# Attention with a gated feed-forward gate on one core: down and output products in whole PSUM banks

## The chip, the core and the metric

The kernel runs on one core of a Trainium2 chip. The metric is device time in microseconds (us) of one execution; the time shown for a kernel is the median of several executions on the same chip, beside which the profile describes one more execution, taken by the hardware profiler. PE is the matrix engine, DVE the vector engine, ACT the activation engine, POOL and SP are used here for small work and for starting transfers.

## What is computed

All inputs are bf16; the sequence has 2048 rows of 640 columns, 32 heads of 20 columns, and a feed-forward width of 1728.

```
xn  = layernorm(x)                         # no weights
q, k, v = split(xn @ wqkv)                 # 32 heads of 20
s   = softmax(q k^T / sqrt(20)) v  @ wo
h   = sigmoid(xn @ w_gate) * (xn @ w_up)
g   = silu(h @ w_down)
out = x + s * g
```

## The kernel before

**Layout.** After a setup that normalises x and transposes it into `xnT`, the queries are cut into four chunks of 512 rows (QC), and the heads into eight groups of four (NG = 8, 32 rows of the partition dimension per head). A pass is one group of heads for one chunk: 32 passes, each of 64 score banks (128 keys x 512 queries of one head, one PSUM bank of 512 fp32 columns). `kT_all` holds K of all groups, 2048 bf16 columns a group; `v_all` holds V.

**Exponentials on two engines.** The 2048 score banks are the bulk of the work. ACT takes two or three banks in one activation (`act_exp`, L1305), out of two sets of PSUM banks. DVE takes single banks: PE writes the scores to one of two banks called `misc0` and `misc1`, DVE clamps them into an SBUF pair (`dy`, L1325), which frees the bank, and when two banks are together it makes the power of two of them with three passes over 1024 columns (L1346, L1350, L1356). The result `p` of either engine is multiplied by V on PE (L1482) into the bank `oacc`. The last group of the last chunk is done in three parts (`PARTS`, `last_job`), with an epilogue that ends the kernel.

**The same two banks serve the jobs.** Everything else that PE does is a job, a generator that asks for a bank, issues its matmuls one at a time into the gaps between scores, and hands DVE or ACT what has to be done with the bank: projections of Q, K and V, `gateup_job` (54 pairs of products into `hT`; the tanh of the gate is on ACT at L679 and the product on DVE at L688, from two banks), `down_job`, `out_job`, `part_job`. At most two jobs are in flight (MOST).

**Who sets the order.** The order of all instructions is made when the program is built: a planner keeps a clock for PE, ACT and DVE (`pe[0]`, `act`, `dve`) from costs written by hand (MM5 = 216 ns for a matmul of 512 columns, MM3 = 136 for 320, 606 for a DVE pass over 512, 400 over 320, 740 over 640), and always issues what would start next. Jobs are sorted by a due time counted in score banks (`STAGE_END`, `OUT_DUE`, `PART_DUE`). A bank is free once the planner's time of the last reader has passed. `issue` and `alone` (from L1240 on) choose whether DVE gets a bank of scores: when a `misc` bank is free and DVE's backlog is under a limit. `zero_add` (L1453 to L1467) issues matmuls on zeros when too little has been streamed by PE in the last 3.4 us of the planner's clock; they go into `oacc` between its own matmuls (L1458), or into a free `misc` bank (L1464). On the chip each engine runs its list in order and waits at semaphores.

**The down product** (`down_job`, L695) runs once for each of 16 tiles of 128 rows, when `hT` of the chunk is whole. Two halves of 320 columns, 14 matmuls each (L709), take one bank after the other; DVE copies each half into `d2` (L713); ACT makes the tanh of all 640 columns (L720, `td`), and DVE makes `gq = (tanh + 1) * d2` (L725). For chunks 0 to 2, POOL starts the write of it to `gq_dram` (L729). In the last chunk it stays, in the memory of K's group t4, which has to be done with by then.

**The output product** (`out_job`, L737) runs for the 12 tiles of chunks 0 to 2, one chunk later. SP starts the load of the gate (L743); two halves, eight matmuls each (L748), take a bank each; DVE multiplies with the gate (L754), and after the second half POOL starts a DMA that adds the tile to `out`, where x was copied before (L757). A tile waits for the tile before it.

**The last chunk.** `part_job` (L767) sums the first five groups' part of the output product in advance, multiplies it with the gate (L787) into `ahead`, which lies in the memory of `hT`, and adds x by a DMA (L790). `near_job` and `last_job` add the last groups.

**The normalisation** of a pass (`normalise`, L796) sends the row sums through memory: POOL starts a write of the sums (L807), a load (L812), after DVE's reciprocal (L816) a write (L817) and four loads (L823); then DVE scales the result (L835).

Of the kernel before, what the change touches and what calls it, by code (L numbers as in the profile page):

```python
# [15 lines left out]
P = 128  # L16
# [42 lines left out]
def kernel(  # L59
# [38 lines left out]
    gq_dram = dram.tile([TT, P, D], FP32, name="gq_dram", tag="gqd")  # L98
# [268 lines left out]
    WINDOW, ENOUGH, ZEROS = 3400.0, 2500.0, 16  # L367
# [327 lines left out]
    def down_job(tt):  # L695
        c, t4 = divmod(tt, QC // P)
        yield "known", lambda: (bulk[0] == NFT and pe[0] > bulk_t[0] + LANDED and len(h_cells.get(c, [])) == NFT and (tt < 2 or tt - 2 in gq_cells)
                                and (c < NQC - 1 or front() >= PER_PASS * (NG * c + t4 + 1)))
        yield "wait", h_cells[c] + ([gq_cells[tt - 2]] if tt > 1 else [])
        hT = hTs[c]  # L700
        d2 = glu[0].tile([P, D], FP32, tag="gqr", bufs=4, name="d2")
        got = []
        for h in range(2):
            e0_, e1_ = h * HALF, (h + 1) * HALF
            held, psd = yield "bank",
            for kf in range(NFT):
                rows = slice(0, P) if kf < NFT - 1 else slice(EDGE * (c % 2), EDGE * (c % 2 + 1))
                h_in = hT[:, kf, :] if kf < NFT - 1 else hEs[c]
                nc.tensor.matmul(psd[:, 0:HALF], lhsT=h_in[rows, t4 * P:(t4 + 1) * P],  # L709
                                 rhs=glu[1][rows, kf, e0_:e1_], start=(kf == 0), stop=(kf == NFT - 1))  # L710
                yield "mm", MM3
            got.append(dve.add(400.0, [Cell(pe[0] + PE_OUT)], lambda psd=psd, e0_=e0_, e1_=e1_:
                               nc.vector.tensor_copy(out=d2[:, e0_:e1_], in_=psd[:, 0:HALF]), 1))  # L713
            give_bank(held, got[-1])
# [3 lines left out]
        def tanh():  # L718
            made["t"] = glu[0].tile([P, D], BF16, tag="td", bufs=1, name="td")
            nc.scalar.activation(out=made["t"], in_=d2, func=ACT.Tanh, scale=0.25)  # L720

        def finish():
            last = c == NQC - 1
            gq = kT_all[:, t4, :].bitcast(FP32)[:, 0:D] if last else d2
            nc.vector.scalar_tensor_tensor(out=gq, in0=made["t"], scalar=1.0, in1=d2, op0=ALU.add, op1=ALU.mult)  # L725
            if last:
                gq_last[t4] = gq
            else:
                nc.gpsimd.dma_start(out=gq_dram[tt, :, :], in_=d2)  # L729
# [3 lines left out]
        gq_cells[tt] = td_free[-1]  # L733

    td_free, tnh_free, gq_cells, out_cells = [], [], {}, {}

    def out_job(tt):  # L737
        qc, t4 = divmod(tt, QC // P)
        yield "known", lambda: (bulk[1] > tt and all((qc, g) in ot_cells for g in range(NG))
                                and (not tt or tt - 1 in out_cells))  # L740
        yield "wait", [ot_cells[qc, g] for g in range(NG)] + ([out_cells[tt - 1]] if tt else [])
        gqr = glu[0].tile([P, D], FP32, tag="gqr", bufs=4, name="gqr")
        nc.sync.dma_start(out=gqr, in_=gq_dram[tt, :, :])  # L743
        landed = Cell(pe[0] + 3000.0)
        for h in range(2):
            held, pss = yield "bank",
            for g in range(NG):
                nc.tensor.matmul(pss[:, 0:HALF], lhsT=oTs[qc, g][:, t4 * P:(t4 + 1) * P],  # L748
                                 rhs=wo_pad[:, g, h * HALF:(h + 1) * HALF], start=(g == 0), stop=(g == NG - 1))
                yield "mm", MM3  # L750

            def finish(h=h, pss=pss):
                half = gqr[:, h * HALF:(h + 1) * HALF]
                nc.vector.scalar_tensor_tensor(out=half, in0=pss[:, 0:HALF], scalar=0.25, in1=half,  # L754
                                               op0=ALU.mult, op1=ALU.mult)
                if h == 1:
                    nc.gpsimd.dma_start(out=out_view[:, tt, :], in_=gqr, accum_op=ALU.add)  # L757

            done = dve.add(400.0, [Cell(pe[0] + PE_OUT), landed], finish, 1)
            give_bank(held, done)  # L760
        out_cells[tt] = done

    gq_last, ahead = {}, []
# [3 lines left out]
    def part_job(t4):  # L767
        tt = (NQC - 1) * 4 + t4
        gqs = range((NQC - 1) * 4, NQC * 4)
        yield "known", lambda: (all((NQC - 1, g) in ot_cells for g in range(PRE))  # L770
                                and all(x in gq_cells for x in gqs) and tt - 1 in out_cells)
        yield "wait", [ot_cells[NQC - 1, g] for g in range(PRE)] + [gq_cells[x] for x in gqs] + [out_cells[tt - 1]]
# [848 lines left out]
```

## Time and profile before

| | |
|---|---|
| median of 3 runs | 883.36 us (883.22 to 884.05) |
| profiled execution | 887.23 us |
| its span, first to last instruction | 885.3 us |
| granted PE clock, mean of the span | 0.996 |
| instructions | 16801 |
| moved by DMA | 63.85 MB |

A group line of the profile reads: line, engine, operation, output and inputs with their shapes, count, then the engine's busy time in the group, the mean ns of one, and the idle time of the engine just before them with what ended it. A row of a stretch gives the stretch's length and then the busy us and, in brackets, the instructions of PE, PE's weight loads (PEld), DVE, ACT and POOL, the granted PE clock (1.00 is full), the share of DMA time and GB/s. A row in the order of time gives start, duration, engine, line and operation, with the idle time before it in square brackets. A duration includes the latency of the instruction, so that neighbours on one engine overlap.

### The profile page before, as it was taken

The page shows a single profiled execution, that of the slowest core. Times are in us where ns is not written, and L with a number is a line of the kernel's source. Part 1 is how long each engine was busy: PE and PEld are TensorE (multiplying, and loading weights), DVE is VectorE, ACT ScalarE, POOL GpSimd, SP SyncE. Part 2 cuts the span into 40 slices and gives each one's busy share as a digit, 9 for nine tenths or more (in the row PEclk, how much of TensorE's full clock was granted, in tenths as well). Part 3 has the DMA queues.
Part 4 walks back from the last instruction along what each step waited for, and adds up shares of the span by engine and source line. Part 5 has one row for each costly group of instructions (what it writes and reads, how often), then busy time and mean ns, then how long its engine had stood idle before and what let it go on. Part 6 is the DMA issues. An engine that isn't in the chain of part 4 may idle for free.

```text
span 885.3 us, 16801 instructions
## 1 busy us (share of the span) xinstructions
PE 806.4 (91%) x6388; PEld 293.1 (33%) x6469; DVE 849.1 (96%) x1210; ACT 864.1 (98%) x828; POOL 158.4 (18%) x299
## 2 busy tenths in 40 slices
PE   7998999899998999999989998999999898999996
PEld 3434333332222333222223332223233232233344
DVE  7799999999999899999999999999999999999997
ACT  7999999999999899999999999999999999999996
POOL 8401111110111112111101132101112021111110
PEclk9999999999999899999999999999999999999999
DMA  8212231115642024223321234312202252200030
GB/s 318 61 51 63 72 106 36 44 55 141 159 131 58 20 83 94 50 58 73 68 56 50 79 66 87 71 38 68 62 29 87 75 86 71 72 22 20 6 69 31
DMA packets 104902, 63.85 MB, mean 72 GB/s; under 512 B 77618, under 2 KB 99206, under 8 KB 104730
## 3 DMA queue, kind: packets, MB, share of 16 engines
q1 hardware_dynamic: 94838, 46.96, 19.7%
q0 software_dynamic: 9984, 15.83, 7.8%
q8 instruction: 50, 0.82, 0.4%
q14 instruction: 30, 0.25, 0.1%
HBM read 49.94 MB, written 16.11 MB: 75 GB/s over the span
## 4 chain that ended last, share of the span: by engine, by line
ACT 52%; issue 17%; DVE 17%; PE 9%; DMA 2%; POOL 1%; SPq 0%; DVEq 0%; ACTq 0%; POOLq 0%
ACT p L1305 49%; DVE dy L1325 4%; DVE p L1356 3%; DVE du L1350 3%; DVE du L1346 3%; PE sc L1279 3%; ACT tnh L679 2%; PE work L709 2%; PE oacc L1482 2%; DMA den<-den_dram 1%; PE work L667 1%; DMA x_sb<-in_A_x_dram 1%; DVE d L713 1%; DVE stats L261 1%; DVE oT L835 1%
## 5 line engine op out<-in xcount | busy, mean ns | idle before, releaser
L1305 ACT ACTIVATE p<-sc 128x1536 bf16<-128x1536 f32 x711 | 818.9, 1344 | 5.7 <-PE sc L1279 3.2
L1279 PE MATMUL sc<-qT,kT_all 21*128 21x512 bf16 (+2 forms) x1892 | 278.5, 370 | 51.7 <-ACT p L1305 46.6
L1325 DVE TENSOR_SCALAR dy<-spare 128x512 f32<-128x512 f32 x271 | 184.8, 682 | 9.2 <-PE spare L1279 7.9
L1279 PEld LDWEIGHTS <-kT_all 21*128 21x128 bf16 x2176 | 89.0, 91 | 290.0 <-issue 278.2
L1346 DVE SCALAR_TENSOR_TENSOR du<-dy 128x1024 f32<-128x1024 uint16 (+1 forms) x170 | 170.1, 1002 | 2.5
L1350 DVE SCALAR_TENSOR_TENSOR du<-du,dy 128x1024 f32<-128x1024 f32 (+1 forms) x166 | 169.1, 1019 | 0.9
L1356 DVE SCALAR_TENSOR_TENSOR p<-du,dy 128x1024 uint16<-128x1024 f32 (+1 forms) x150 | 166.7, 1111 | 1.0
L1482 PE MATMUL oacc<-p,v_all 128*21 128x512 bf16 (+2 forms) x2176 | 157.2, 371 | 0.5 <-issue 0.3
L1279 PE MATMUL spare<-qT,kT_all 21*128 21x512 bf16 (+2 forms) x284 | 104.0, 374 | 1.7 <-DVE dy L1325 0.8
L807 POOL DMA_DIRECT2D den_dram<-oev x30 | 17.4, 582 | 368.2 <-DVE oev L803 357.2
L667 PE MATMUL work<-xnT,wg 128*128 128x512 bf16 (+1 forms) x262 | 73.3, 382 | 3.7 <-DVE dy L1325 1.0
L709 PE MATMUL work<-wd,hT 128*128 128x320 bf16 x416 | 74.7, 306 | 1.6 <-DVE dy L1325 0.9
L667 PE MATMUL work<-xnT,wu 128*128 128x512 bf16 (+1 forms) x265 | 70.7, 381 | 2.9 <-DVE dy L1325 1.2
L823 POOL DMA_DIRECT2D rl<-rec_dram x120 | 60.7, 535 | 54.7 <-DMA rec_dram<-den 47.8
L1458 PE MATMUL oacc<-xnT,zero 128*128 128x512 bf16 x147 | 50.9, 386 | 2.8 <-issue 2.5
L1482 PEld LDWEIGHTS <-v_all 128*21 128x21 bf16 x2176 | 31.9, 90 | 59.6 <-issue 56.3
L709 PEld LDWEIGHTS <-hT 128*128 128x128 bf16 x416 | 34.6, 99 | 37.2 <-issue 26.5
L817 POOL DMA_DIRECT2D rec_dram<-den x30 | 16.4, 548 | 129.6 <-DVE den L816 129.6
L679 ACT ACTIVATE tnh<-work 128x512 bf16<-128x512 f32 x54 | 37.6, 696 | 0.0
L667 PEld LDWEIGHTS <-wu 128*128 128x128 bf16 (+1 forms) x280 | 23.8, 98 | 38.0 <-issue 20.2
L688 DVE SCALAR_TENSOR_TENSOR hT<-tnh,work 128x512 bf16<-128x512 bf16 x52 | 35.3, 678 | 0.3 <-ACT tnh L679 0.2
L748 PE MATMUL work<-wo_pad,oT 128*128 128x320 bf16 x192 | 34.3, 301 | 0.8 <-DVE dy L1325 0.5
(133 smaller groups left out, 579.1 us busy)
## 6 DMA issues: line engine op xcount, KB each, us to landing
wg<-in_B_w_gate_dram SPq DMA_DIRECT2D x52, 160.0 KB
wu<-in_B_w_up_dram SPq DMA_DIRECT2D x52, 160.0 KB
rl<-rec_dram POOLq DMA_DIRECT2D x120, 64.0 KB, 2.4
qT<-q_dram SPq DMA_DIRECT2D x31, 128.0 KB
gq_dram<-d POOLq DMA_DIRECT2D x12, 320.0 KB, 2.5
gqr<-gq_dram SPq DMA_DIRECT2D x12, 320.0 KB
kT_all<-k_dram SPq DMA_DIRECT2D x28, 128.0 KB
wd<-in_B_w_down_dram SPq DMA_DIRECT2D x13, 160.0 KB
```

Of the source, the lines that this page charges most:

```text
L667: nc.tensor.matmul(ps[EDGE * k:EDGE * (k + 1), :] if both else ps, lhsT=w[:, kd, 0:EDGE if both else P], rhs=xnT[:, kd, (c + k) * QC:(c + ...
L679: nc.scalar.activation(out=made["t"][0:fsz, :], in_=psg[0:fsz, :], func=ACT.Tanh, scale=0.5)
L709: nc.tensor.matmul(psd[:, 0:HALF], lhsT=h_in[rows, t4 * P:(t4 + 1) * P], rhs=glu[1][rows, kf, e0_:e1_], start=(kf == 0), stop=(kf == NFT - 1))
L823: nc.gpsimd.dma_start(out=t["rl"][32 * j:32 * j + 32, :], in_=rec_dram[n, j:j + 1, :].to_broadcast([32, QC]))
L1279: nc.tensor.matmul(ps[:, c0:c0 + n], lhsT=kT_all[rows, g, kt * P:(kt + 1) * P], rhs=qTs[qc, g][rows, q0:q0 + n], start=True, stop=True, ti ...
L1305: nc.scalar.activation(out=buf.tile(), in_=ps, func=ACT.Exp, bias=EXP_BIAS, scale=exp_scale)
L1325: nc.vector.tensor_scalar(out=pair.y[:, i * 512:(i + 1) * 512], in0=ps, scalar1=LEAST, scalar2=None, op0=ALU.max)
L1346: nc.vector.scalar_tensor_tensor(out=t["u"][:, a:e], in0=t["f"][:, a:e], scalar=CUBE_2, in1=t["f"][:, a:e], op0=ALU.add, op1=ALU.mult)
L1350: nc.vector.scalar_tensor_tensor(out=t["u"][:, a:e], in0=t["u"][:, a:e], scalar=CUBE_1, in1=t["f"][:, a:e], op0=ALU.add, op1=ALU.mult)
L1356: nc.vector.scalar_tensor_tensor(out=t["p"][:, a:e], in0=t["u"][:, a:e], scalar=CUBE_SCALE, in1=t["y"][:, a:e], op0=ALU.mult, op1=ALU.add)
L1458: nc.tensor.matmul(oacc, lhsT=zero, rhs=xnT[:, 0, 0:QC], start=not begun, stop=not begun, skip_group_check=True)
L1482: nc.tensor.matmul(oacc[32 * j:32 * j + 1 + Dh, q0:q0 + width], lhsT=v_all[:, kt, GH * g + j, 0:1 + Dh], rhs=buf.ap[:, i, c0:c0 + width], ...
```

## The change

The down and the output product are cut into banks instead of tiles. The four tiles of a chunk have 4 x 640 = 2560 columns side by side, which are five banks of 512; `down_pieces(k)` lists which columns of which tiles fall into bank k (one piece of 512; 128 + 384; 256 + 256; 384 + 128; 512). For each of 20 banks `down_job(c, k)` issues 14 matmuls for each piece, ACT makes the tanh straight from PSUM, and DVE makes the gate from the tanh and PSUM; the copies and `d2` are gone, and the bank is given back after the gate. `td` shares the buffers of the gate-up's `tnh`. Before, a job waited for the gate of two tiles earlier; now it doesn't. The output product has 15 banks instead of 24 halves; the gate is loaded by banks (`gq_dram` has the new shape), the planner lets 1.4 us pass after the load is started before it asks for a bank, and each piece is added to `out` by a DMA of its own.

In the last chunk the gates (`gq_last`) fill the first 10 KB a partition of K's memory (groups 0 to 2), and `ahead` the next 10 KB (groups 2 to 4), no longer `hT`'s memory; `part_job` may start one pass earlier, waits only for the gates of its own tile, and is due 24 banks earlier. `zero_add` takes a `misc` bank only when it has been free for 400 ns of the planner's clock. The planner's costs follow.

```diff
-    gq_dram = dram.tile([TT, P, D], FP32, name="gq_dram", tag="gqd")
+    gq_dram = dram.tile([NQC, P, 4 * D], FP32, name="gq_dram", tag="gqd")
...
-    WINDOW, ENOUGH, ZEROS = 3400.0, 2500.0, 16
+    WINDOW, ENOUGH, ZEROS, RESTED = 3400.0, 2500.0, 16, 400.0
...
-            yield "known", lambda: len(d_cells.get(c - 1, [])) == QC // P
+            yield "known", lambda: len(d_cells.get(c - 1, [])) == D // P
...
+    def mm_time(n):
+        return max(n / 2.4 + 3.0, 100.0)
+
+    def down_pieces(k):
+        return [(t4, max(t4 * D, k * QC), min((t4 + 1) * D, (k + 1) * QC)) for t4 in range(QC // P)
+                if t4 * D < (k + 1) * QC and (t4 + 1) * D > k * QC]
+
+    def down_job(c, k):
+        last = c == NQC - 1
+        yield "known", lambda: (bulk[0] == NFT and pe[0] > bulk_t[0] + LANDED and len(h_cells.get(c, [])) == NFT
+                                and (not last or front() >= PER_PASS * (NG * c + k // 2 + 1)))
+        yield "wait", h_cells[c]
...
+        held, psd = yield "bank",
+        for t4, f0, f1 in down_pieces(k):
             for kf in range(NFT):
...
+                nc.tensor.matmul(psd[:, f0 - k * QC:f1 - k * QC], lhsT=h_in[rows, t4 * P:(t4 + 1) * P],
+                                 rhs=glu[1][rows, kf, f0 - t4 * D:f1 - t4 * D], start=(kf == 0), stop=(kf == NFT - 1),
+                                 skip_group_check=True)
+                yield "mm", mm_time(f1 - f0), (f1 - f0) / 2.4
...
-            made["t"] = glu[0].tile([P, D], BF16, tag="td", bufs=1, name="td")
-            nc.scalar.activation(out=made["t"], in_=d2, func=ACT.Tanh, scale=0.25)
+            made["t"] = wk.tile([P, QC], BF16, tag="tnh", bufs=2, name="td")
+            nc.scalar.activation(out=made["t"], in_=psd, func=ACT.Tanh, scale=0.25)
...
-            nc.vector.scalar_tensor_tensor(out=gq, in0=made["t"], scalar=1.0, in1=d2, op0=ALU.add, op1=ALU.mult)
...
+            nc.vector.scalar_tensor_tensor(out=gq, in0=made["t"], scalar=1.0, in1=psd, op0=ALU.add, op1=ALU.mult)
+            if not last:
+                nc.gpsimd.dma_start(out=gq_dram[c, :, k * QC:(k + 1) * QC], in_=gq)
...
-        turned = act.add(590.0, got + td_free[-1:], tanh, 0, EXP_LAG)
-        td_free.append(dve.add(740.0, [turned], finish, 2))
+        turned = act.add(480.0, [Cell(pe[0] + PE_OUT + 100.0), *tnh_free[-2:-1]], tanh, 0, EXP_LAG)
+        tnh_free.append(dve.add(606.0, [turned], finish, 1))
+        give_bank(held, tnh_free[-1])
...
+    def out_job(qc, k):
+        cut = down_pieces(k)
...
+        nc.sync.dma_start(out=gqr, in_=gq_dram[qc, :, k * QC:(k + 1) * QC])
         landed = Cell(pe[0] + 3000.0)
+        yield "wait", [Cell(pe[0] + 1400.0)]
+        held, pss = yield "bank",
+        for t4, f0, f1 in cut:
             for g in range(NG):
...
+            nc.vector.scalar_tensor_tensor(out=gqr, in0=pss, scalar=0.25, in1=gqr, op0=ALU.mult, op1=ALU.mult)
+            for t4, f0, f1 in cut:
+                nc.gpsimd.dma_start(out=out_view[:, qc * 4 + t4, f0 - t4 * D:f1 - t4 * D],
+                                    in_=gqr[:, f0 - k * QC:f1 - k * QC], accum_op=ALU.add)
...
+    gq_last = kT_all[:, 0:3, :].rearrange("p g s -> p (g s)").bitcast(FP32)[:, 0:4 * D]
+    ahead = kT_all[:, 0:5, :].rearrange("p g s -> p (g s)").bitcast(FP32)[:, 4 * D:8 * D].rearrange(
+        "p (t d) -> p t d", d=D)
...
-    GU_COST, DOWN_COST = 10 * MM5, 2 * NFT * MM3
-    OUT_COST, PART_COST = 2 * NG * MM3, 2 * (NG - 3) * MM3
-    PART_DUE = [LAST-24 + 8 * t4 for t4 in range(4)]
+    GU_COST, DOWN_COST = 10 * MM5, NFT * (MM5 + 10.0)
+    OUT_COST, PART_COST = NG * (MM5 + 10.0), 2 * (NG - 3) * MM3
+    PART_DUE = [LAST-48 + 8 * t4 for t4 in range(4)]
...
-        jobs.append(Job(part_job(t4), PART_COST, len(steps) - 2, PART_DUE[t4]))
+        jobs.append(Job(part_job(t4), PART_COST, len(steps) - 3, PART_DUE[t4]))
...
-            free = [i for i in range(2) if banks[i].t is not None and banks[i].t <= pe[0]]
+            free = [i for i in range(2) if banks[i].t is not None and banks[i].t <= pe[0] - RESTED]
```

More of the change, by code (lines that the diff above doesn't have):

```diff
@@ L693, in gateup_job @@
             h_cells.setdefault(c + k, []).append(tnh_free[-1])
[L695 to L699, printed above, removed]
-        hT = hTs[c]
[L701 to L705, printed above, removed]
+    def mm_time(n):
[8 more added lines that the diff above has]
+        yield "wait", h_cells[c]
+        hT = hTs[c]
+        if last:
+            gq = gq_last[:, k * QC:(k + 1) * QC]
+        else:
+            gq = glu[0].tile([P, D], FP32, tag="gqr", bufs=4, name="gq")[:, 0:QC]
+        held, psd = yield "bank",
+        for t4, f0, f1 in down_pieces(k):
             for kf in range(NFT):
@@ new lines, in finish @@
+            if not last:
[3 more added lines that the diff above has]
+        give_bank(held, tnh_free[-1])
+        gq_cells[c, k] = tnh_free[-1]
+    tnh_free, gq_cells, out_cells = [], {}, {}
+    def out_job(qc, k):
+        cut = down_pieces(k)
+        yield "known", lambda: (bulk[1] > qc * 4 + cut[-1][0] and all((qc, g) in ot_cells for g in range(NG)))
+        yield "wait", [ot_cells[qc, g] for g in range(NG)]
+        gqr = glu[0].tile([P, D], FP32, tag="gqr", bufs=4, name="gqr")[:, 0:QC]
+        nc.sync.dma_start(out=gqr, in_=gq_dram[qc, :, k * QC:(k + 1) * QC])
@@ L827, in s4 @@
         def s4():
-            if g >= 3 and qc and not all(out_cells.get(tt, Cell()).t for tt in range((qc - 1) * 4, qc * 4)):
+            if g >= 3 and qc and not all(out_cells.get((qc - 1, k), Cell()).t for k in range(D // P)):
                 at(pe[0] + 300.0, s4)
```

74 lines of the change are left out of this document (21 added, 53 removed).

## The prediction

> **What bounds the kernel now.** I read the busy shares first, then the shares of the chain of waits that ended last.
>
> ```profile
> span 885.3 us, 16801 instructions
> ...
> PE 806.4 (91%) x6388; PEld 293.1 (33%) x6469; DVE 849.1 (96%) x1210; ACT 864.1 (98%) x828; POOL 158.4 (18%) x299
> ...
> ACT 52%; issue 17%; DVE 17%; PE 9%; DMA 2%; POOL 1%; SPq 0%; DVEq 0%; ACTq 0%; POOLq 0%
> ```
>
> ACT stands idle for 21 us of 885.3 and holds half of the chain; DVE, idle for 36 us, comes next. Then the busy time of each engine in stretches of 22 us (columns: PE, PEld, DVE, ACT, POOL, granted clock, DMA):
>
> ```profile
> 264.00:286.00 22.00, 19.26 (x145) 6.20 (x140) 21.79 (x26) 22.00 (x23) 3.69 (x7) 1.00 0.29 65
> 286.00:308.00 22.00, 20.43 (x151) 6.70 (x153) 18.79 (x24) 19.52 (x18) 2.77 (x6) 0.84 0.07 16
> ...
> 352.00:374.00 22.00, 20.27 (x154) 5.95 (x159) 20.33 (x26) 21.26 (x21) 4.90 (x8) 1.00 0.30 50
> ...
> 726.00:748.00 22.00, 19.45 (x143) 6.04 (x145) 20.02 (x26) 21.09 (x22) 3.15 (x7) 1.00 0.38 79
> ```
>
> The first row is the ordinary one: ACT 22.00 of 22.00, DVE within 0.2 us of full. ACT loses 2.48 us in the second, where the granted clock falls, 0.74 in the third, 0.91 in the fourth. So nearly every microsecond is an ACT microsecond. But the planner may give an exponential to either engine: ACT takes two or three score banks at a time (L1305), DVE one (L1325 to L1356). A microsecond freed on DVE therefore counts, at the rate at which banks can be exchanged. The groups of ACT by shape, and then of DVE:
>
> ```profile
> L1305 ACT ACTIVATE p<-sc 128x1536 bf16<-128x1536 f32 x355 | 552.5, 1556 | 2.0 <-PE sc L1279 1.5 <-PE spare L1279 0.4
> L1305 ACT ACTIVATE p<-sc 128x1024 bf16<-128x1024 f32 x356 | 402.6, 1131 | 3.7 <-PE spare L1279 1.8 <-PE sc L1279 1.7
> L679 ACT ACTIVATE tnh<-work 128x512 bf16<-128x512 f32 x54 | 37.6, 696 | 0.0
> L720 ACT ACTIVATE td<-d 128x640 bf16<-128x640 f32 x16 | 12.1, 754 | 1.4 <-DVE d L713 1.1
> ```
>
> ```profile
> L1325 DVE TENSOR_SCALAR dy<-spare 128x512 f32<-128x512 f32 x271 | 184.8, 682 | 9.2 <-PE spare L1279 7.9
> ...
> L688 DVE SCALAR_TENSOR_TENSOR hT<-tnh,work 128x512 bf16<-128x512 bf16 x52 | 35.3, 678 | 0.3 <-ACT tnh L679 0.2
> ...
> L713 DVE COPY d<-work 128x320 f32<-128x320 f32 x32 | 15.4, 482 | 0.0
> ...
> L754 DVE SCALAR_TENSOR_TENSOR gqr<-work,gqr 128x320 f32<-128x320 f32 x24 | 11.5, 478 | 0.0
> L725 DVE SCALAR_TENSOR_TENSOR d<-td,d 128x640 f32<-128x640 bf16 x12 | 9.8, 817 | 0.0
> ```
>
> One bank less on ACT is 1556 - 1131 = 425 ns. Durations on DVE overlap, so I price its work from start to start, in the order of time:
>
> ```profile
> 311.01 0.82 DVE L725 SCALAR_TENSOR_TENSOR d<-td,d 128x640 f32<-128x640 bf16 x1
> 311.75 0.68 DVE L1325 TENSOR_SCALAR dy<-spare 128x512 f32<-128x512 f32 x1
> 312.35 0.48 DVE L713 COPY d<-work 128x320 f32<-128x320 f32 x1
> 312.75 0.68 DVE L1350 SCALAR_TENSOR_TENSOR du<-du,dy 128x512 f32<-128x512 f32 x1
> ```
>
> ```profile
> 351.40 1.21 DVE L1350 SCALAR_TENSOR_TENSOR du<-du,dy 128x1024 f32<-128x1024 f32 x1
> 352.53 0.48 DVE L754 SCALAR_TENSOR_TENSOR gqr<-work,gqr 128x320 f32<-128x320 f32 x1
> ```
>
> 640 columns take 0.74 us, 512 take 0.60, 320 take 0.40, 1024 take 1.13. A bank of exponentials on DVE is 0.60 and half of three passes over 1024, 0.60 + 1.70 = 2.30 us.
>
> **The change part by part. DVE, down product.** Removed: 32 copies at 0.40 and 16 gates of 640 at 0.74 = 24.6 us. Added: 20 gates of 512 with one operand in PSUM. That shape with that operand is L688 (678 ns, as long as L1325's 0.68), so 0.60 each, 12.0 us. Saved 12.6 us.
>
> **DVE, output product.** 24 x 0.40 = 9.6 us become 15 x 0.60 = 9.0. Saved 0.6. Together 13.2 us, certain in count, but worth only what the planner makes of them. If it fills them with x more banks and the run shortens by d: 2.30 x = 13.2 - d and d = 0.425 x, so x = 4.8 and d = 2.0 us. The bounds are 0 (no free bank when DVE is free) and 2.0; I take 2.0, because DVE is full in the ordinary stretch, so the planner already finds a bank whenever DVE has room.
>
> **ACT.** 16 activations of 640 become 20 of 512. From start to start:
>
> ```profile
> 291.41 0.79 ACT L679 ACTIVATE tnh<-work 128x512 bf16<-128x512 f32 x1
> ...
> 291.89 4.83 ACT L1305 ACTIVATE p<-sc 128x1024 bf16<-128x1024 f32 x4
> ```
>
> ```profile
> 309.82 0.73 ACT L720 ACTIVATE td<-d 128x640 bf16<-128x640 f32 x1
> 310.44 3.70 ACT L1305 ACTIVATE p<-sc 128x1536 bf16<-128x1536 f32 x3
> ```
>
> 20 x 0.48 = 9.6 against 16 x 0.62 = 9.9: 0.3 saved. The new activation waits for PE instead of for DVE's copies. In ACT's groups above L720 cost ACT 1.4 us of idling (1.1 for the copies), L679, which waits for PE, none in 54; so 1.4 goes, and behind it on ACT only the next exponentials are queued. 1.7 us of ACT, shared with DVE at 2.30 / (2.30 + 0.425) = 0.84, is 1.4 us of time. Bounds: 0 if PE is as late as the copies were, 1.4 if never; I take 1.2.
>
> **PE.** The columns and the number of matmuls stay: eight pieces a chunk by 14 or 8 operands. Widths change from 320 to 512, 384, 256 and 128. A width of 128 with full weights isn't in these loops. Its nearest row is 160 wide.
>
> ```profile
> L709 PE MATMUL work<-wd,hT 128*128 128x320 bf16 x416 | 74.7, 306 | 1.6 <-DVE dy L1325 0.9 <-DVE d L713 0.2 <-DVE du L1350 0.2
> ...
> L1458 PE MATMUL oacc<-xnT,zero 128*128 128x512 bf16 x147 | 50.9, 386 | 2.8 <-issue 2.5 <-DVE oev L803 0.2
> ...
> L164 PE MATMUL work<-wv,xnT 128*128 128x160 bf16 x140 | 13.7, 234 | 0.1
> ```
>
> 13.7 / 140 = 98 ns bounds it above; 2/5 of L709's 74.7 / 416 = 180 ns, 72, below. 4 x 28 + 3 x 16 = 160 such pieces cost at most 160 x 26 ns = 4.2 us of PE. Its cover is 50.9 us of matmuls on zeros (L1458) which only keep PE busy and make way; so nothing, and 4.2 us if that cover were gone.
>
> **Banks.** A down piece now keeps its bank through ACT and DVE, about 0.5 + 0.6 us and their queues, where a copy gave it back after 0.4. It is done 20 times, not 32; the output product takes 15 banks for 24 and no longer sits in one while its gate lands. Nothing to me; if the planner misjudges, PE stands at a matmul whose bank isn't free, and the scores queued behind it, on which ACT waits, are late. That is the second rival.
>
> **Queues.** POOL issues 15 writes of the gate for 12 and 24 accumulating writes for 12 (pieces cut at tile borders); SP 15 loads for 12. The bytes stay. The loads' new wait of 1.4 us is the planner's: it holds one of two job places and blocks no instruction. What counts on POOL is what queues behind:
>
> ```profile
> 353.32 0.88 POOL L757 DMA_DIRECT2D out_dram<-gqr  x1 [1.55 <-DVE gqr L754]
> 353.90 0.87 POOL L812 DMA_DIRECT2D den<-den_dram  x1
> ```
>
> ```profile
> 353.90 5.53 DMA den<-den_dram
> ```
>
> ```profile
> den<-den_dram POOLq DMA_DIRECT2D x30, 8.0 KB, 2.1
> ```
>
> The normalisation's small load, 2.1 us in the median, took 5.53 right behind an accumulating write, and DVE's reciprocal stopped for it; the second row is its twin in a later chunk:
>
> ```profile
> 359.45 0.25 DVE L816 RECIPROCAL den<-den 128x16 f32<-128x16 f32 x1 [1.54 <-DMA den<-den_dram]
> ```
>
> ```profile
> 729.74 0.25 DVE L816 RECIPROCAL den<-den 128x16 f32<-128x16 f32 x1 [1.91 <-DMA den<-den_dram]
> ```
>
> These are the third and fourth of the stretches above: ACT lost 0.74 + 0.91 = 1.65 us. (The Trainium skill, page "DMA: Bandwidth & Descriptors", section "Issuing engines are not separate DMA queues", says that transfers of all issuers share the same 16 engines and interleave; by that the bytes decide and the price stays 1.65; the row shows a place in line that costs.) Twice the instructions could cost another 1.65; equal bytes, 0. I take +0.6.
>
> **Last chunk.** Its partial sums no longer wait for hT's memory but for K's first groups, and move up by 24 banks of scores. They end before the last 27 us either way:
>
> ```profile
> L787 DVE SCALAR_TENSOR_TENSOR hT<-work,kT_all x8: 429/483/486, 834.8 to 854.8; 128x320 f32<-128x320 f32 x8
> ```
>
> The work is the same and DVE is full at both places: 0, at most the 8 x 0.40 = 3.2 us of DVE at the exchange rate of 2.0 / 13.2, 0.5 us either way.
>
> **The zero matmuls that must find a bank rested for 0.4 us.** This is the stretch with the lower clock:
>
> ```profile
> 294.03 0.38 PE L1464 MATMUL unused<-xnT,zero 128*128 128x512 bf16 x1 [0.47 <-DVE hE L688]
> ```
>
> ```profile
> 293.00:294.00 1.00, 0.39 (x3) 0.19 (x3) 1.00 (x3) 1.00 (x2) 0.00 (x0) 1.00 0.00 0
> ...
> 295.00:296.00 1.00, 0.78 (x6) 0.39 (x4) 1.00 (x3) 1.00 (x2) 0.45 (x1) 0.50 0.00 0
> ...
> 301.00:302.00 1.00, 1.00 (x7) 0.31 (x6) 0.34 (x1) 0.32 (x1) 0.00 (x0) 0.85 0.00 0
> ```
>
> PE stood 0.47 us before a zero matmul whose bank DVE was still reading; in that microsecond it was busy 0.39, then the clock was halved until 301, and ACT lost its 2.48 us. The change forbids this very zero matmul. If the dip goes, 2.48 x 0.84 = 2.1 us go with it. I don't count it: the profiled execution took 887.23 us (1.9 more than its span) and the median is 883.36; those 3.9 us may be the profile's own cost, or the dip in part, which the median runs then hadn't. So 0, at best -2.1.
>
> **Sum.** -2.0 - 1.2 + 0.6 = -2.6 us on the profiled execution, 884.6; the same taken from the median gives 880.8.
>
> **The rivals.** First, the dip was in all runs and goes: -4.7, 878.7 from the median. For it: its trigger is edited. Against: one low stretch need not halve the clock in each run. Chance 0.17.
>
> Second, slower: longer holds make new dips. A down job waits for its bank until ACT and DVE are through; should that chain be later than planned, PE stands still, as for 0.47 us at 293.5, the clock halves for about 7 us, and ACT loses 2.48 us, 2.1 us of time. One new dip gives 882.9, no change; it decides from three on, with 6.3 - 2.6 = +3.7 us, 887.1; four chunks offer the places. Against it: the gate-up's second bank already waits for ACT and then DVE, 54 times, with this one dip. (The Trainium skill, page "TensorE: Matmul & The Clock Gate", section "A second HAM failure mode: psum-queue depth-cycling", says that cycling through PSUM banks makes PE pause briefly so often that its clock swings; that speaks against longer holds, and the row at 293 agrees in kind.) Chance 0.18, with the doubled POOL stalls in it.
>
> Third, the change shortens DVE's list but the planner can't use it: two banks serve both the jobs and DVE's exponentials, so the 13.2 us become DVE idling. Then -1.2 + 0.6 = -0.6: 882.8. For it: DVE idles 36 us already. Chance 0.22, with one new dip counted here.
>
> **How the numbers follow.** Forecast 880.8, chance 0.43. About 0.2%, 1.8 us, is what a measurement of this kernel can tell from no change, so faster means below 881.6: 0.43 + 0.17 = 0.60. Within is the third rival, 0.22, slower the second, 0.18. The range reaches from below the first rival with the full POOL saving (878.7 - 0.6 and 0.5 of the last chunk: 877.6) to the second, 887.1.
>
> **What the profile would show.** Right: no copies at the down product, 20 gates near 680 ns and 15 output gates; four to six more L1325 than 271 and ACT's exponentials shorter by as many banks; DVE's busy share unchanged; no ACT idling at the down activation. Wrong: L1325's count the same with DVE's idling up by ten microseconds (third rival); stretches with a clock below 1.00 during down jobs (second); L816 waiting for more than 4 us in all (the POOL term). Since the planner lays out all instructions anew, a shift of where jobs fall can move stalls of a microsecond either way, which no row of before can show.

## The result, and the profile after

| | before | changed |
|---|---|---|
| median of 6 runs each | 883.70 us (883.05 to 884.97) | 880.88 us (879.49 to 882.74) |
| ratio, 95% interval | | 0.9964 (0.9953 to 0.9975) |
| profiled execution, its span | 887.23, 885.3 | 882.74, 881.0 |
| profiled once more (e11, e12), its span | 884.00, 882.1 | 879.94, 878.2 |

The changed kernel is faster by 0.36%, 2.8 us by the medians. First the busy shares of its profile and the shares of its chain of waits:

```profile
span 881.0 us, 16760 instructions
...
PE 802.5 (91%) x6358; PEld 286.1 (32%) x6440; DVE 840.6 (95%) x1164; ACT 862.3 (98%) x832; POOL 170.0 (19%) x314
...
ACT 62%; issue 19%; PE 9%; DVE 8%; DMA 1%; POOL 1%; SPq 0%; ACTq 0%; DVEq 0%; POOLq 0%
```

DVE is busy 8.5 us less, yet its idle time rose from 36 to 40 us. ACT's idle time fell from 21 to 19, and the chain now runs through ACT where it ran through DVE: 62% and 8% against 52% and 17%. Then the stretches of 22 us of the changed kernel, the four that were shown of before:

```profile
264.00:286.00 22.00, 19.26 (x145) 6.20 (x140) 21.79 (x26) 22.00 (x23) 3.68 (x7) 1.00 0.28 66
286.00:308.00 22.00, 20.16 (x156) 6.23 (x154) 20.22 (x27) 20.73 (x20) 2.80 (x6) 0.92 0.07 17
...
352.00:374.00 22.00, 19.74 (x151) 6.29 (x150) 20.75 (x28) 21.50 (x21) 7.11 (x11) 1.00 0.31 38
...
726.00:748.00 22.00, 20.12 (x139) 6.15 (x143) 21.25 (x27) 22.00 (x22) 3.12 (x6) 1.00 0.33 78
```

ACT loses 1.27 us in the second (2.48 before), 0.50 in the third (0.74), none in the fourth (0.91). The dip of the clock is still there, with half its weight. Then the groups by shape: ACT, DVE and PE of the changed kernel (lines below the edit are one higher: L1326 is the old L1325).

```profile
L1306 ACT ACTIVATE p<-sc 128x1536 bf16<-128x1536 f32 x355 | 562.1, 1583 | 1.4 <-PE sc L1280 1.2 <-PE spare L1280 0.2
L1306 ACT ACTIVATE p<-sc 128x1024 bf16<-128x1024 f32 x356 | 412.1, 1158 | 3.0 <-PE sc L1280 2.8 <-PE spare L1280 0.2
...
L726 ACT ACTIVATE td<-work 128x512 bf16<-128x512 f32 x20 | 14.7, 737 | 0.0
```

```profile
L1326 DVE TENSOR_SCALAR dy<-spare 128x512 f32<-128x512 f32 x271 | 184.8, 682 | 13.7 <-PE spare L1280 12.0
...
L757 DVE SCALAR_TENSOR_TENSOR gqr<-work,gqr 128x512 f32<-128x512 f32 x15 | 10.2, 682 | 0.0
L729 DVE SCALAR_TENSOR_TENSOR gq<-td,work 128x512 f32<-128x512 bf16 x15 | 10.2, 680 | 0.0
...
L729 DVE SCALAR_TENSOR_TENSOR kT_all<-td,work 128x512 f32<-128x512 bf16 x5 | 3.4, 684 | 0.5 <-ACT td L726 0.4
```

```profile
L1459 PE MATMUL oacc<-xnT,zero 128*128 128x512 bf16 x124 | 42.9, 387 | 3.0 <-issue 2.4 <-DVE oev L804 0.6
...
L717 PE MATMUL work<-wd,hT 128*128 128x128 bf16 x104 | 9.4, 221 | 0.6 <-DVE dy L1326 0.6
```

The tanh waits for nothing (L726, 0.0). The gates and the output gates have the forecast counts and lengths. But DVE has 271 banks as before, ACT the same 355 + 356 activations, and DVE idles 13.7 us in front of L1326 where it idled 9.2. So the engines share the exponentials as before, and DVE's freed time was not spent on banks as forecast.

**An undisturbed pair.** Both profiles above have half-clock windows near 294 us, and the changed kernel has one more, at 506. Therefore both kernels were profiled again (e11 before, e12 changed), and in neither does the clock fall anywhere before the last 3 us. These rows of the stretch from 286, first e11 and then e12, stand for it:

```profile
286.00:308.00 22.00, 20.55 (x174) 7.62 (x172) 21.64 (x29) 21.85 (x21) 3.68 (x7) 1.00 0.11 28
```

```profile
286.00:308.00 22.00, 20.08 (x170) 6.63 (x168) 21.60 (x29) 22.00 (x21) 4.22 (x8) 1.00 0.13 32
```

The groups of ACT and DVE of e11, and then of e12 (shapes of L1305 and L1306 put together, so that the means are over both; a mean is of durations, which overlap):

```profile
L1305 ACT ACTIVATE p<-sc 128x1536 bf16<-128x1536 f32 x711 | 818.5, 1346 | 3.1 <-PE sc L1279 1.5 <-PE spare L1279 1.3
L720 ACT ACTIVATE td<-d 128x640 bf16<-128x640 f32 x16 | 12.1, 754 | 1.4 <-DVE d L713 1.1
L1325 DVE TENSOR_SCALAR dy<-spare 128x512 f32<-128x512 f32 x271 | 184.5, 681 | 6.5 <-PE spare L1279 5.1
```

```profile
L1306 ACT ACTIVATE p<-sc 128x1536 bf16<-128x1536 f32 x711 | 822.8, 1376 | 2.0 <-PE sc L1280 1.8 <-PE spare L1280 0.2
L726 ACT ACTIVATE td<-work 128x512 bf16<-128x512 f32 x20 | 15.0, 752 | 0.0
L1326 DVE TENSOR_SCALAR dy<-spare 128x512 f32<-128x512 f32 x271 | 184.3, 680 | 11.3 <-PE spare L1280 9.6
```

From 882.1 to 878.2 are 3.9 us. I added up ACT's line of both traces from its first exponential on, each instruction counted to the start of the next. ACT's idle time falls from 4.75 to 2.06 us, -2.7 (of it 1.3 in front of the tanh); the exponentials from 806.0 to 805.0, -1.0; the tanhs from 36.2 to 35.4, -0.8; the end after the last activation grows by 0.5; the rest is rounding and the setup. On DVE, counted in the same way, the copies and gates fall from 24.7 + 9.5 to 12.0 + 9.0: the 13.2 us of the prediction. Of these 4.8 turn up as idle time (27.2 to 32.0) and 3.6 in longer exponentials (642.6 to 646.2 for the same 271 banks: an instruction with a gap behind it counts whole, since nothing overlaps its end). So of the 3.9 us on ACT's line 2.1 belong to the tanh, 1.3 of waiting and 0.8 of length.

Runs with a clock near full agree with this pair better than with the medians: the changed kernel's three with a granted clock of 0.998 or more took 879.49, 879.75 and 881.13 us, the kernel before, in its 41 such runs beside the experiments, 884.1 in the median. So with the clock near full the change is worth about 4 us, though three runs are few. The 2.8 us of the medians are less because the changed kernel's other three runs stood at 0.995 or 0.996.

### The profile page after: what moved, and what is told of

Its sections match the earlier page's. It is cut to its first block, busy times and chain, and to the rows that moved or that the text cites. A ratio compares the mean times of both kernels' runs of the same rounds, so it can differ in the third digit from the quotient of the medians.

```text
span 881.0 us, 16760 instructions
## 1 busy us (share of the span) xinstructions
PE 802.5 (91%) x6358; PEld 286.1 (32%) x6440; DVE 840.6 (95%) x1164; ACT 862.3 (98%) x832; POOL 170.0 (19%) x314
## 4 chain that ended last, share of the span: by engine, by line
ACT 62%; issue 19%; PE 9%; DVE 8%; DMA 1%; POOL 1%; SPq 0%; ACTq 0%; DVEq 0%; POOLq 0%
ACT p L1306 59%; PE sc L1280 3%; ACT tnh L679 2%; DVE dy L1326 2%; PE work L667 1%; DVE du L1351 1%; PE oacc L1483 1%; DVE du L1347 1%; DVE p L1357 1%; PE work L717 1%; ACT td L726 1%; DMA x_sb<-in_A_x_dram 1%; DVE stats L261 1%; PE oacc L1459 1%; DMA den<-den_dram 0%
## 5 line engine op out<-in xcount | busy, mean ns | idle before, releaser
L1306 ACT ACTIVATE p<-sc 128x1536 bf16<-128x1536 f32 x711 | 822.8, 1370 | 4.4 <-PE sc L1280 4.0
L1326 DVE TENSOR_SCALAR dy<-spare 128x512 f32<-128x512 f32 x271 | 184.8, 682 | 13.7 <-PE spare L1280 12.0
L717 PE MATMUL work<-wd,hT 128*128 128x512 bf16 (+3 forms) x410 | 77.1, 306 | 2.5 <-DVE dy L1326 1.5
L1459 PE MATMUL oacc<-xnT,zero 128*128 128x512 bf16 x124 | 42.9, 387 | 3.0 <-issue 2.4
L717 PEld LDWEIGHTS <-hT 128*128 128x128 bf16 x416 | 31.1, 98 | 40.8 <-issue 32.4
L138 PE MATMUL work<-xnT,wqd 128*120 128x512 bf16 (+1 forms) x115 | 35.0, 393 | 0.6 <-DVE hT L688 0.3
```

The source lines that it names most:

```text
L717: nc.tensor.matmul(psd[:, f0 - k * QC:f1 - k * QC], lhsT=h_in[rows, t4 * P:(t4 + 1) * P], rhs=glu[1][rows, kf, f0 - t4 * D:f1 - t4 * D], s ...
L1306: nc.scalar.activation(out=buf.tile(), in_=ps, func=ACT.Exp, bias=EXP_BIAS, scale=exp_scale)
L1326: nc.vector.tensor_scalar(out=pair.y[:, i * 512:(i + 1) * 512], in0=ps, scalar1=LEAST, scalar2=None, op0=ALU.max)
L1459: nc.tensor.matmul(oacc, lhsT=zero, rhs=xnT[:, 0, 0:QC], start=not begun, stop=not begun, skip_group_check=True)
```

## The experiments

Three theories were held against each other. **A**, the chain: the time came from ACT, which no longer waits for DVE's copies. **B**, DVE's time: what counts is how much work DVE has, and 12 us of it are worth some microseconds wherever they are taken. **C**, the layout: the planner lays out all instructions anew after any edit, and the new layout happens to be better.

### e1: the down product alone

```diff
 # before, with the changed kernel's mm_time, down_pieces, down_job and gq_last
...
-        nc.sync.dma_start(out=gqr, in_=gq_dram[tt, :, :])
+        nc.sync.dma_start(out=gqr, in_=gq_dram[qc, :, t4 * D:(t4 + 1) * D])
```

> The kernel before with the down product alone in whole banks (gate straight from PSUM); the output product stays in halves of 320, the last chunk's partial sums and the zero matmuls as before. Theory A (ACT no longer waits for DVE's copies and is starved less): nearly the whole gain, 2 to 4 us below before, ACT idle by about 3 us less. Theory B (the 12.6 us of DVE freed are exchanged for shorter ACT work): 2.0 us below before, DVE's banks above 271. Theory C (any edit re-lays the plan, and the 2.8 us are its luck): anywhere within 3 us of before.

Measured: 880.48 us in the median of 6, ratio to before 0.9953 (0.9939 to 0.9967), against 0.9964 (0.9953 to 0.9975) for the whole change. Its profile has 271 banks on DVE as well, and 1.1 + 2.3 us of ACT idling before the exponentials where before had 2.0 + 3.7. The output product in banks, the partial sums in K's memory and the rested bank add nothing that can be measured.

### e2: DVE's time given back, and the planner told

```diff
+            def again():
+                nc.vector.tensor_tensor(out=gq, in0=gq, in1=gq, op=ALU.max)
+            gq_cells[c, k] = dve.add(606.0, [tnh_free[-1]], again, 1)
```

(The write of the gate to memory starts after this pass.) Twenty passes of 0.6 us, 12 us.

> The changed kernel with one more DVE pass over each gate of the down product (gate = max(gate, gate), 20 passes of 512 columns, 12 us of DVE; the planner knows them; no bank, no ACT work and no job waits longer, only the gate's way to memory). Theory A: 0 to 0.5 us above the changed kernel, the passes fill DVE's idling. Theory B: 2.0 us above it, with four to five fewer banks on DVE. Theory C: anywhere within 3 us.

Measured: 887.71 us in the median of 11, ratio 1.0046 (1.0030 to 1.0062), so 0.8% above the changed kernel. Its groups of ACT and DVE:

```profile
L1309 ACT ACTIVATE p<-sc 128x1536 bf16<-128x1536 f32 x713 | 824.3, 1362 | 5.2 <-PE spare L1283 2.5 <-PE sc L1283 2.2
L1329 DVE TENSOR_SCALAR dy<-spare 128x512 f32<-128x512 f32 x267 | 182.0, 682 | 12.9 <-PE spare L1283 10.1 <-PE sc L1283 1.8
```

Here the planner does exchange: four banks fewer on DVE for 12 us. But ACT's idle time before the exponentials is 5.2 us as well, and the whole costs 7 us, not the 2 of the exchange. None of the three theories had put it that high.

### e3: the chain given back

```diff
...
+        copied = dve.add(606.0, [Cell(pe[0] + PE_OUT)], lambda: nc.vector.tensor_copy(out=d2, in_=psd), 1)
+        give_bank(held, copied)
-        turned = act.add(480.0, [Cell(pe[0] + PE_OUT + 100.0), *tnh_free[-2:-1]], tanh, 0, EXP_LAG)
+        turned = act.add(480.0, [copied, *tnh_free[-2:-1]], tanh, 0, EXP_LAG)
...
```

(The tanh and the gate read `d2`; the bank is given back after the copy.)

> The changed kernel, but DVE copies each whole bank of the down product to SBUF (20 copies of 512, 12 us), gives the bank back, ACT's tanh waits for the copy, and the gate is made from SBUF: the old chain in whole banks. Same DVE work as the run with the extra pass. Theory A: 1 to 2 us above that run, with ACT idle before the tanh by 1 us or more in all. Theory B: the same as that run within 0.5 us. Theory C: anywhere within 3 us.

Measured: 886.34 us in the median of 12, ratio 1.0023 (1.0011 to 1.0035). ACT and DVE in its profile:

```profile
L724 ACT ACTIVATE td<-gq 128x512 bf16<-128x512 f32 x20 | 13.6, 678 | 1.8 <-DVE gq L731 1.6
...
L1325 DVE TENSOR_SCALAR dy<-spare 128x512 f32<-128x512 f32 x270 | 183.8, 681 | 11.8 <-PE spare L1279 10.5
```

The wait is back (1.8 us in front of the tanh), with the same 12 us on DVE as in e2; and the kernel isn't slower than e2. The wait costs nothing on top of DVE's time, unless the earlier return of the bank pays for it. That speaks for B against A, as far as two plans can be compared (e7 shows how far).

### e4: halves of 320, but straight from PSUM

```diff
...
-                               nc.vector.tensor_copy(out=d2[:, e0_:e1_], in_=psd[:, 0:HALF]), 1))
...
+                nc.scalar.activation(out=made["t"], in_=psd[:, 0:HALF], func=ACT.Tanh, scale=0.25)
...
+                nc.vector.scalar_tensor_tensor(out=gq[:, e0_:e1_], in0=made["t"], scalar=1.0, in1=psd[:, 0:HALF], op0=ALU.add, op1=ALU.mult)
```

> The kernel before in its halves of 320 columns, but tanh and gate straight from PSUM without copies (32 tanh and 32 gates of 320; DVE saves 11.8 us as in the change, ACT gains 0.5 us of work). Theory A: 1 to 2.5 us below before, since the wait for the copies goes whatever the width. Theory B: 1.7 us below before, with four more banks on DVE. If whole banks are what counts: no change.

Measured: 881.67 us in the median of 7, ratio 0.9965 (0.9952 to 0.9978). Without any whole banks the gain is that of the change. It has 273 banks on DVE and no dip of the clock; its tanhs, 32 of 0.32 us start to start, cost ACT as much as the 16 before (10.3 and 10.2 us). A and B both fit it; whole banks as the cause don't.

### e5 and e6: another backlog limit

```diff
-    BUFS, D_BACKLOG = {"p3": 4, "p2": 4, "p1": 2}, 3600
+    BUFS, D_BACKLOG = {"p3": 4, "p2": 4, "p1": 2}, 3800
```

One edit of the limit under which DVE is given a bank, which leaves the computation as it is (what the planner makes of it, how many banks each engine gets and how many zero matmuls, may move); e5 is the changed kernel, e6 the one before.

> The changed kernel with the planner's limit of DVE's backlog at 3800 for 3600: an edit with no purpose but to have the plan laid out anew. Theory A (ACT's waits) and B (DVE's freed time): as the changed kernel within 1 us, and 2 to 4 us under the kernel before with the same edit. Theory C (luck of the plan): 1 to 4 us off the changed kernel, and on either side of its twin.

> The kernel before with the same limit at 3800. Theories A and B: as before within 1 us, so 2 to 4 us above its changed twin. Theory C: 1 to 4 us off before, most likely above it, since the kernel's constants were set for the plan that it has.

Measured: e5 881.28 us (10 runs), ratio 0.9975 (0.9956 to 0.9994); e6 886.70 (10 runs), ratio 1.0034 (1.0006 to 1.0062). The pair differs by 5.4 us. The profiled run of e6 took 897.37 us, with a dip that this row in stretches of 21 us shows (clock 0.51 nearly from end to end):

```profile
520.00:541.00 21.00, 19.50 (x91) 4.45 (x90) 13.82 (x18) 12.73 (x11) 3.45 (x6) 0.51 0.21 43
```

### e7 and e8: one nanosecond in the planner's costs

```diff
-    MM5, MM3, MM1 = 216.0, 136.0, 70.0
+    MM5, MM3, MM1 = 215.0, 136.0, 70.0
```

> The changed kernel with the planner's price of a 512 column matmul at 215 ns for 216: again an edit with no purpose. Theories A and B: as the changed kernel within 1 us. Theory C: 1 to 4 us off it.

> The kernel before with the same price at 215 ns. Theories A and B: as before within 1 us and 2 to 4 us above its changed twin. Theory C: off before by 1 to 4 us, and the difference to the twin anywhere from 3 us slower to 6 us faster.

Measured: e7 885.02 us (10 runs), ratio 0.9999 (0.9986 to 1.0013); e8 885.24 (10 runs), ratio 1.0007 (0.9990 to 1.0024). The pair differs by 0.2 us. So an edit that changes nothing of the computation moves the median of the changed kernel by 0.4 or 4.1 us, and that of the one before (884.35 in its runs beside these four) by 2.4 or 0.9. C has a case: the layout alone is as large as the result. The three pairs give -2.8, -5.4 and -0.2 us, none of them a loss, about -2.8 in the mean. (Part of the spread is the clock again: among runs at 0.998 or more the medians are 881.2 and 885.3 in the pair of e5 and e6, 883.4 and 884.4 in that of e7 and e8, which is -4.1 and -1.0.) It also means that e1 to e4, each with a plan of its own, can't tell theories apart that differ by a microsecond or two.

The counts of banks on DVE are 272 and 269 in e5 and e6, 273 and 270 in e7 and e8. So in these two plans the changed kernel does put three more banks on DVE, of the 4.8 forecast; but the two pairs with the same exchange differ by 5.4 and 0.2 us, and the pair with none by 2.8, so the exchange isn't what sets the gain.

To get free of the layout, the next two kernels keep the order of all other instructions and change only how long DVE is at work. The traces bear it out: apart from the added passes, the instructions of every engine stand in the same order in e9 as in the changed kernel, and in e10 as in the one before.

### e9: DVE's time given back, the order kept

```diff
             nc.vector.scalar_tensor_tensor(out=gq, in0=made["t"], scalar=1.0, in1=psd, op0=ALU.add, op1=ALU.mult)
+            nc.vector.tensor_tensor(out=gq, in0=gq, in1=gq, op=ALU.max)
```

(The planner's cost stays at 606, so that it doesn't know.)

> The changed kernel with the extra DVE pass of 512 columns over each of the 20 gates (12 us of DVE), of which the planner knows nothing: every engine's list keeps the order of the changed kernel, so no new plan comes in. Theory B (DVE's time counts by itself at the exchange rate or by delay): 2 us or more above the changed kernel. Theory A (DVE has slack behind a fixed order): under 1 us above it. Theory C says that the 6.8 us of the run with the planned extra pass came from its new plan: here under 2 us.

Measured: 890.36 us in the median of 4 (888.20 to 891.52), ratio 1.0054 (1.0034 to 1.0075) against 0.9964: 0.9%, 8 us, for 12 us of DVE. A part of it is clock, 0.992 to 0.996 in its four runs; but its run at 0.996 took 888.20, the two of the changed kernel at 0.996 took 880.63 and 881.17, so about 7 us are left. Its exponentials on ACT, and then, from the waits, who PE waited for (total, times, longest), in e9 and in the changed kernel:

```profile
L1307 ACT ACTIVATE p<-sc 128x1536 bf16<-128x1536 f32 x711 | 823.9, 1343 | 9.2 <-PE sc L1281 8.5 <-PE spare L1281 0.2
```

```profile
PE work L717 <- DVE dy L1327: 2.5, 6, 0.7
...
PE work L752 <- DVE dy L1327: 1.6, 5, 0.5
```

```profile
PE work L717 <- DVE dy L1326: 1.5, 4, 0.7
...
PE work L751 <- DVE dy L1326: 0.2, 1, 0.2
```

This is the path, for time that is added. DVE clamps a bank late (dy), so the bank comes free late; PE stands at the first matmul of a job for that bank (L717, L752); the scores are queued behind it, and ACT waits for the scores, 8.5 us where it waited 4.0 in the changed kernel. (Three half-clock windows lie in this profile, two in that of the changed kernel. Without these and the microsecond behind each, ACT's waits before its exponentials are 5.1 us in e9 and 1.9 in the changed kernel.) The two lines shown are the largest but not all: from 28 us on, the waits of PE that DVE ended add up to 12.0 us in e9 and 6.6 in the changed kernel; most of the rest of the rise are the output product's multiplications (gqr) and the results of DVE's exponentials (p).

### e10: DVE's time taken from the kernel before, the order kept

```diff
-            nc.vector.scalar_tensor_tensor(out=gq, in0=made["t"], scalar=1.0, in1=d2, op0=ALU.add, op1=ALU.mult)
+            nc.vector.scalar_tensor_tensor(out=gq[:, 0:HALF], in0=made["t"][:, 0:HALF], scalar=1.0, in1=d2[:, 0:HALF], op0=ALU.add, op1=ALU.mult)
...
-                nc.vector.scalar_tensor_tensor(out=half, in0=pss[:, 0:HALF], scalar=0.25, in1=half,
+                nc.vector.scalar_tensor_tensor(out=half[:, 0:32], in0=pss[:, 0:32], scalar=0.25, in1=half[:, 0:32],
```

(The 16 gates, four of them in the last chunk, fall from 11.8 to 6.8 us, start to start, and the 24 multiplications from 9.5 to 2.5: 12 us less on DVE. Half of the gate's columns and nine tenths of the multiplication's are left out. Copies, waits, matmuls and transfers stay; the shorter multiplication also gives its bank back some 0.3 us earlier.)

> The kernel before in its own order, with about the DVE time taken away that the change saves: the gate of the down product is made on 320 of 640 columns (16 x 0.34 us less) and the output product's multiplication on 32 of 320 columns (24 x 0.30 us less), 12.6 us in all, so those columns of the result are not computed. The copies stay, and ACT waits for them as before. Theory A: within 0.5 us of before, since ACT's list is the same and it still waits for the copies. Theory B: 1 to 2 us below before. Theory C: as before within 1 us, because the gain is in a new order.

Measured: 882.37 us in the median of 6, ratio 0.9967 (0.9955 to 0.9980). Its profiled run has a span of 881.9 us and one half-clock window at 531.7:

```profile
L1305 ACT ACTIVATE p<-sc 128x1536 bf16<-128x1536 f32 x711 | 819.0, 1353 | 3.1 <-PE sc L1279 2.0 <-PE spare L1279 0.9
L720 ACT ACTIVATE td<-d 128x640 bf16<-128x640 f32 x16 | 12.2, 765 | 1.0 <-DVE d L713 0.7
L1325 DVE TENSOR_SCALAR dy<-spare 128x512 f32<-128x512 f32 x271 | 184.6, 681 | 13.3 <-PE spare L1279 12.1
```

The order is that of before, the 271 banks too, and the tanh still waits 1.0 us. By the medians nearly the whole gain is there, 0.33 of 0.36%. At a clock of 0.998 or more it is less: its four such runs took 881.72 to 882.58 us, those of before beside them 884.06 to 885.34, so 2 to 3 us of the 4. PE's waits that DVE ended fall from 8.9 us in e11 (the kernel before, without a dip) to 7.5 here and 6.5 in e12 (the changed kernel, without a dip), in the direction of the path of e9. So half of the gain or more needs neither a better layout nor the shorter chain, and no exchange of banks: less work on DVE is enough. What the rest comes from isn't separated; on ACT's line of the undisturbed pair the tanh has 2.1 us of it.

### e11 and e12: both kernels profiled again

> The kernel before, profiled once more. If the dip of the clock at 294 us depends on where the windows of the clock's control fall in this execution, the dip starts elsewhere or is absent, ACT idles up to 2.2 us less in that stretch, and the execution takes 883 to 885 us instead of 887.2. If the dip belongs to the program, it stands at 294 us again.

> The changed kernel, profiled once more. If the two dips at 294 and 506 us depend on the windows, they move or vanish and the execution takes 880 to 881 us; if they belong to the program, both stand again, with 882 to 883 us.

Measured: 884.00 and 879.94 us, one run each; the rows stand in the first section. Without dips on either side the change is worth 3.9 us of span.

## Why the prediction was right, and the step that failed

The time was forecast as 880.8 and is 880.88. That the two agree to 0.1 us is luck: another plan moves the time by up to 4 us, and with the clock near full the gain is about 4 us, not 2.6. One of its terms came about in another way, some of the others were off.

**DVE, the 13.2 us: right. What they are worth: right in size, wrong in how.** The step that failed is "x = 4.8 and d = 2.0 us", with its reason that "DVE is full in the ordinary stretch, so the planner already finds a bank whenever DVE has room". The count is 271 before and after. I had named as the sign of the third rival, with 882.8, the count unchanged and DVE's idle time up by ten microseconds. The first half came, the second only in part (27.2 to 32.0), and the rival doesn't hold either: e10 idles DVE still more (37 us counted in the same way, 27 in e11), exchanges nothing, and is 0.33% faster. I had assumed that a freed microsecond is either spent on a bank or lost. There is a third use: DVE is less often late with a clamp, and the bank, PE's next job, the scores and ACT follow. In e9 the waits show this path; for the gain they only point the same way (8.9, 7.5, 6.5 us). Nor is it symmetric: 12 us less are worth 2 to 3 us (e10, in before's order), 12 us more cost 7 to 8 (e9, in the changed order). The second is far above the 12 / 13.2 x 2.0 = 1.8 of the exchange; e2, where the planner could exchange and did, pays 7 (its PE waits for DVE add up to only 5.8 us, so e2 pays in another way than e9). Why adding costs so much more than taking away brings is not shown; it fits that both engines are near full, so that late banks pile up, while the first engine to catch up gains nothing more.

**ACT, -1.2: in the profile, its worth open.** The idle 1.4 us in front of the tanh is gone (L726, 0.0) and the tanhs are 0.8 us shorter from start to start, where I had 0.3. So ACT's line gains 2.1 us where I had 1.7. e10 keeps 1.0 us of the wait and has half of the gain or more, and e3 has the wait and no loss beyond e2's, in a plan of its own. What these microseconds are worth alone, the 0.84 each that I had or less, wasn't separated from DVE's.

**PE, nothing: right.** The pieces of 128 columns take 9.4 / 104 = 90 ns, counted as the bounds were, within my 72 to 98. The zero matmuls that gave way fell from 147 to 124 records, 50.9 to 42.9 us.

**Banks held longer, nothing: right, no sign of the second rival.** In e12 there is no dip at all. The dips that other profiles have are at other places from run to run, in kernels with copies (before, e6, e8) as well as without. Of the kernels without copies (changed, e1, e4, e5, e7, e12), 7 of 40 runs have a granted clock of 0.996 or less, of those with copies (before, e6, e8, e11) 22 of 84; where DVE has an extra pass (e2, e3, e9) it is 18 of 27. The Trainium skill ("TensorE: Matmul & The Clock Gate", section "A second HAM failure mode: psum-queue depth-cycling") describes a kernel that cycles through PSUM banks, whose short pauses of PE between groups of matmuls make its clock swing. I had taken longer holds for more such pauses; these runs don't show more dips from them.

**POOL, +0.6: wrong in sign here.** The rows of the changed kernel: the reciprocal's wait, and the accumulating writes.

```profile
DVE den L817 <- DMA den<-den_dram: 1.2, 1, 1.2
```

```profile
L759 POOL DMA_DIRECT2D out_dram<-gqr x24 | 21.1, 992 | 31.8 <-DVE gqr L757 31.8
```

DVE waits for the small load once, 1.2 us, against 3.7 in three waits before, 1.54 + 1.91 of them in the rows that I had: at 729 the stop is gone, and ACT is full there (22.00). Twice the instructions kept POOL 11.6 us longer at work (158.4 to 170.0) and stopped nobody more. I had priced a place in line by how many stand in it, while it seems to be the load's moment that decides, whether one of them is just ahead of it: with the same 24 writes, DVE waits 3.3 us for that load in e2 and 0.2 in e3. That wasn't tried by itself. In e1, where these writes are as before, the time is the same within what two plans can tell.

**Last chunk, 0: right** within what e1 can tell.

**The dip at 294 us, 0: right that it doesn't go, wrong in its price.** The zero matmul at 294.03 is gone. In its place, PE waits at the same point for ACT, with twice the idle time:

```profile
294.49 0.58 PE L1280 MATMUL sc<-qT,kT_all 21*128 21x512 bf16 x3 [0.95 <-ACT p L1306]
```

And the clock falls at 294.6. In e11 the same zero matmul stands there, with the same wait, and the clock doesn't fall:

```profile
293.81 0.38 PE L1464 MATMUL unused<-xnT,zero 128*128 128x512 bf16 x1 [0.46 <-DVE hE L688]
```

So the zero matmul isn't what triggers it, and the first rival falls: the dip is in some executions of either kernel. Its price I had as 2.1 us for 7 us of half clock. Between the two profiles of before, with a dip of 6.8 us and without, lie 885.3 - 882.1 = 3.2 us, between those of the changed kernel, with two windows of 3.4, 881.0 - 878.2 = 2.8. This also explains part of the 3.9 us between the profile of before and its median, which I had left open.

**What stays open.** How much the change would bring in yet another layout: the three pairs span 0.2 to 5.4 us, and three can't tell a mean to better than a few microseconds. That the gain isn't luck alone rests on e9 and e10, which keep the order. What the tanh's shorter way is worth, and how the gain splits between the two, would take a kernel in before's order with the tanh read from PSUM and DVE's time left as it is.

## What to carry to other kernels

When two engines share a kind of work, time freed on the second one needn't be exchanged to count; it counts when its lateness is what holds buffers, so ask who waits for its outputs, and test it by adding or leaving out a pass with the order unchanged. When a planner lays out the program, compare a change of a few tenths of a per cent over several neutral layouts: here one nanosecond in a cost moved the time by 4 us. And profile a kernel twice before explaining a stretch by its clock, and compare executions of equal clock.

## What the runs showed of the hardware

**The dips come in steps of 3.41 us, and the same program has them or not.** Their lengths in the traces are 3.41, 6.83 and 20.48 us, one, two and six times 3.413, at half the clock. The Trainium skill says this ("TensorE: Matmul & The Clock Gate", section "What's actually happening"): the rate is set per window of 3413 ns, the windows run free of the program's start, and the factor is a half or whole; the traces agree. What the windows' free run would explain here: ten of the profiles (before, changed, e1 to e4, e9 to e12) hold the same instructions up to 293.9 us, and four of them have the dip there. In these four, the first window of full clock begins 3.85 to 4.54 us after the first instruction, in the six without it 4.98 to 6.21 us after it. So it seems to depend on how the windows lie over PE's pauses there, half a microsecond to one; that is read from the ten and wasn't tried.

**One such window costs this kernel 1.4 to 1.6 us** (3.2 us for two, 2.8 us for two). The longest, of six windows in e6, is the row shown there: ACT busy for 12.73 of 21 us, while PE, busy for 19.50, got through 91 matmuls, where the changed kernel's rows of 22 us have 139 to 156. With two windows more at 397.6, that run of 897.37 was 12 us above e6's three runs at a clock of 0.998 (884.92 to 885.55), 1.5 us a window.
